# Cross-covariance attention and channel mix: all engines in a hand-written, step-by-step woven order

## The chip, the cores and the metric

One core of one Trainium2 chip. The metric is the device time of one execution in microseconds (us). All runs that are quoted were fast (none was over 1.5% above the fastest of its kernel). The granted clock is the share of its full clock that PE was given, as the profile records it. PE is the matrix engine (TensorE), PEld its weight loads, ACT ScalarE, DVE VectorE, POOL GpSimd.

## The reference, cut to what matters

Four batches of 6208 tokens with 256 channels; the hidden width of the channel mix is 1024.

```python
# attention over channels: q, k, v are [4, 6208, 256]
qn = q / (norm(q, axis=1, keepdims=True) + 1e-6)      # norm over tokens
kn = k / (norm(k, axis=1, keepdims=True) + 1e-6)
a  = softmax(kn.transpose(0, 2, 1) @ qn / tau)        # [4, 256, 256]
x  = v @ a
# channel mix with a token shift
x_prev = x shifted by one token, 0 in front
xk = mu_k * x + (1 - mu_k) * x_prev;  xr = mu_r * x + (1 - mu_r) * x_prev
k  = maximum(xk @ w_k, 0)                             # "up", 256 -> 1024
v  = (k * k) @ w_v                                    # "down", 1024 -> 256
out = sigmoid(xr @ w_r) * v
```

A batch must have its whole covariance (q, k) and its softmax before its first x. So a batch's covariance is made while the blocks of the batch before it run through the channel mix.

## The kernel before

Each batch has 12 blocks of 512 tokens; the 64 tokens left over in each batch are treated together, once. The order below is what is *written*. The framework's scheduler then decides in which order each engine runs it, within the dependencies.

```python
def cov_group(b, g):                       # 512 tokens of q and k: one "group of rows"
    ...
    if b == 0:                             # first batch: f32 loads, cast on DVE
        qk_f = pq.tile([P, S, 2, C], F32, name="qk_f", tag="qk_f")      # 4 buffers
        for i in range(2):
            nc.sync.dma_start(qk_f[:rows, :n, i, :], src[i])            # 1 KB pieces
        nc.vector.tensor_copy(qk[:rows, :n], qk_f[:rows, :n])
        nc.scalar.activation(qk2[:rows, :n], qk_f[:rows, :n], AF.Square)
    else:                                  # later batches: casting software loads (POOL)
        for i in range(2):
            nc.gpsimd.dma_start(qk[:rows, :n, i, :], src[i])
        nc.scalar.activation(qk2[:rows, :n], qk[:rows, :n], AF.Square)  # 2048 columns
    for s in range(n):                     # one "row": 1024 matmul columns
        nc.tensor.matmul(ssq_ps, ones[:rows], qk2[:rows, s]..., ...)
        for ih in range(2):
            nc.tensor.matmul(s_ps[:, ih, :], qk[:rows, s, 1, ...], qk[:rows, s, 0, :], ...)

def channel_mix(xk, xr, m, store):
    for fh in range(8):                    # up
        kT_ps = ps.tile([P, M], F32, name="kT_ps", tag="kT_ps", bufs=2)
        for dh in range(2):
            nc.tensor.matmul(kT_ps[:, :m], w_k_sb[...], xk[:, dh, :m], ...)
        if fh == 7:
            nc.vector.tensor_relu(kr[:, :m], kT_ps[:, :m])
        else:
            nc.scalar.activation(kr[:, :m], kT_ps[:, :m], AF.Relu)
        nc.vector.tensor_tensor(kk[:, fh, :m], kr[:, :m], kr[:, :m], op=OP.mult)
    for s in range((m + P - 1) // P):      # down and gate
        vr_ps = ps.tile([P, 2 * D], F32, name="vr_ps", tag="vr_ps", bufs=2)
        # 2 matmuls with w_r_sb, 8 with w_v_sb
        nc.scalar.activation(res[:ms, s], vr_ps[:ms, D:], AF.Sigmoid)
        nc.vector.tensor_tensor(res[:ms, s], res[:ms, s], vr_ps[:ms, :D], op=OP.mult)
    store(res)

for g in range(NB + 1):
    cov_group(0, g)
load_weights()
...
cov_softmax(0)
for i, (b, t) in enumerate(blocks):
    ...
    project(b, vs.pop(i), xT, carry)       # transposes of v, x = v @ a
    xk, xr = mix(xT, M)
    if b + 1 < B and t < NB - 1:
        cov_group(b + 1, t)                # next batch's rows
        ...
    channel_mix(xk, xr, M, store_block(b, t))
    if b + 1 < B and t == NB - 2:
        cov_softmax(b + 1)
```

Of the kernel before, what the change touches and what calls it, by code (L numbers as in the profile page):

```python
# [10 lines left out]
F32 = mybir.dt.float32  # L11
# [7 lines left out]
def kernel(  # L19
# [31 lines left out]
    ps = ctx.enter_context(tc.tile_pool(name="ps", bufs=1, space=bass.MemoryType.PSUM))  # L51

# [12 lines left out]
    a_sb = const.tile([P, B, 2, C], BF16, name="a_sb")  # L65

    def load_weights():
        nc.sync.dma_start(mu_k_t, moe_mu_k.rearrange("(h p) -> p h", p=P))
        nc.sync.dma_start(mu_r_t, moe_mu_r.rearrange("(h p) -> p h", p=P))
        nc.gpsimd.dma_start(w_k_sb, moe_w_k.rearrange("(ko ki) f -> ki ko f", ki=P))  # L70
        nc.gpsimd.dma_start(w_r_sb, moe_w_r.rearrange("(ko ki) d -> ki ko d", ki=P))
        nc.gpsimd.dma_start(w_v_sb, moe_w_v.rearrange("(fo fi) d -> fi fo d", fi=P))


    cov = {}

    def cov_group(b, g):

        if g == 0:
            cov[b] = (ps.tile([P, 2, C], F32, name="s_ps", tag="s_ps"),  # L80
                      ps.tile([P, 2 * C], F32, name="ssq_ps", tag="ssq_ps"))
        s_ps, ssq_ps = cov[b]
        full = g < NB
        n = S if full else 1
        rows = P if full else L
        src = []
        for t in (q, k):
            if full:
                src.append(t[b, :NB * M, :].rearrange("(p j) c -> p j c", p=P)[:, g * S:(g + 1) * S, :])
            else:  # L90
                src.append(t[b, NB * M:, :].rearrange("(p j) c -> p j c", j=1))
        qk = pq.tile([P, S, 2, C], BF16, name="qk", tag="qk")
        qk2 = pq.tile([P, S, 2, C], BF16, name="qk2", tag="qk2", bufs=3)
        if b == 0:
            qk_f = pq.tile([P, S, 2, C], F32, name="qk_f", tag="qk_f")
            for i in range(2):
                nc.sync.dma_start(qk_f[:rows, :n, i, :], src[i])  # L97
            nc.vector.tensor_copy(qk[:rows, :n], qk_f[:rows, :n])  # L98
            nc.scalar.activation(qk2[:rows, :n], qk_f[:rows, :n], AF.Square)
        else:  # L100
            for i in range(2):
                nc.gpsimd.dma_start(qk[:rows, :n, i, :], src[i])  # L102
            nc.scalar.activation(qk2[:rows, :n], qk[:rows, :n], AF.Square)
        for s in range(n):
            t0 = g == 0 and s == 0
            te = g == NB
            nc.tensor.matmul(ssq_ps, ones[:rows], qk2[:rows, s].rearrange("p i c -> p (i c)"),  # L107
                             start=t0, stop=te)
            for ih in range(2):
                nc.tensor.matmul(s_ps[:, ih, :], qk[:rows, s, 1, ih * P:(ih + 1) * P],  # L110
                                 qk[:rows, s, 0, :], start=t0 and ih == 0, stop=te,
                                 skip_group_check=True)

    def cov_softmax(b):
        s_ps, ssq_ps = cov.pop(b)
        nrm = pn.tile([P, 2 * C], F32, name="nrm")
        nc.scalar.activation(nrm, ssq_ps, AF.Sqrt)
        junk = pn.tile([P, P], F32, name="junk")
        rk = pn.tile([P, 2], F32, name="rk")
        for ih in range(2):  # L120
            nc.vector.scalar_tensor_tensor(junk, nrm[:, C + ih * P:C + (ih + 1) * P], 1.0, ident_f,
                                           op0=OP.mult, op1=OP.mult, accum_out=rk[:, ih:ih + 1])
        nc.vector.tensor_scalar_add(nrm[:, :C], nrm[:, :C], 1e-6)
        rq = pn.tile([P, C], F32, name="rq")
        nc.vector.reciprocal(rq, nrm[:, :C])
        nc.vector.tensor_scalar_add(rk, rk, 1e-6)
        nc.vector.reciprocal(rk, rk)
        if inv_tau != 1.0:
            nc.vector.tensor_scalar_mul(rk, rk, inv_tau)
        s_sb = pn.tile([P, 2, C], F32, name="s_sb")  # L130
        nc.vector.tensor_tensor(s_sb, s_ps, rq.unsqueeze(1).to_broadcast([P, 2, C]), op=OP.mult)
        for ih in range(2):
            nc.vector.tensor_scalar_mul(s_sb[:, ih], s_sb[:, ih], rk[:, ih:ih + 1])
        mx = pn.tile([P, 2], F32, name="mx")
        nc.vector.tensor_reduce(mx, s_sb, axis=AX, op=OP.max, negate=True)
        sm = pn.tile([P, 2], F32, name="sm")
        for ih in range(2):
            nc.scalar.activation(s_sb[:, ih], s_sb[:, ih], AF.Exp, bias=mx[:, ih:ih + 1],
                                 accum_out=sm[:, ih:ih + 1])
        nc.vector.reciprocal(sm, sm)  # L140
        for ih in range(2):
            nc.vector.tensor_scalar_mul(a_sb[:, b, ih, :], s_sb[:, ih], sm[:, ih:ih + 1])


    def load_v(b, t):
        v_bf = p2.tile([P, S, C], BF16, name="v_bf", tag="v_bf", bufs=4)
        nc.gpsimd.dma_start(v_bf, v[b, t * M:(t + 1) * M, :].rearrange("(s p) c -> p s c", p=P))  # L147
        return v_bf

    def mix(xT, m):  # L150

        delta = p2.tile([P, 2, M], BF16, name="delta", tag="delta")
        xk = p2.tile([P, 2, M], BF16, name="xk", tag="xk")
        xr = p2.tile([P, 2, M], BF16, name="xr", tag="xr")
        nc.vector.tensor_tensor(delta[:, :, :m], xT[:, :, 1:m + 1], xT[:, :, :m], op=OP.subtract)  # L155
        for mu, o in ((mu_k_t, xk), (mu_r_t, xr)):
            for dh in range(2):
                nc.vector.scalar_tensor_tensor(o[:, dh, :m], delta[:, dh, :m], mu[:, dh:dh + 1],  # L158
                                               xT[:, dh, :m], op0=OP.mult, op1=OP.add)
        return xk, xr  # L160

    def project(b, v_bf, xT, carry):

        vT_ps = ps.tile([P, 2, M], BF16, name="vT_ps", tag="vT_ps")
        for ch in range(2):
            for s in range(S):
                nc.tensor.transpose(vT_ps[:, ch, s * P:(s + 1) * P], v_bf[:, s, ch * P:(ch + 1) * P], ident)  # L167
        vT = p2.tile([P, 2, M], BF16, name="vT", tag="vT", bufs=2)
        nc.vector.tensor_copy(vT, vT_ps)  # L169
        for dh in range(2):  # L170
            xT_ps = ps.tile([P, M], F32, name="xT_ps", tag="xT_ps")
            for ih in range(2):
                nc.tensor.matmul(xT_ps, a_sb[:, b, ih, dh * P:(dh + 1) * P], vT[:, ih, :],  # L173
                                 start=ih == 0, stop=ih == 1)
            nc.scalar.copy(xT[:, dh, 1:], xT_ps)  # L175
        if carry is None:
            nc.gpsimd.memset(xT[:, :, 0:1], 0.0)
        else:
            nc.gpsimd.tensor_copy(xT[:, :, 0:1], carry)  # L179

    def channel_mix(xk, xr, m, store):
        kk = p2.tile([P, 8, M], BF16, name="kk", tag="kk", bufs=2)
        for fh in range(8):
            kT_ps = ps.tile([P, M], F32, name="kT_ps", tag="kT_ps", bufs=2)
            for dh in range(2):
                nc.tensor.matmul(kT_ps[:, :m], w_k_sb[:, dh, fh * P:(fh + 1) * P], xk[:, dh, :m],  # L186
                                 start=dh == 0, stop=dh == 1)
            kr = p2.tile([P, M], BF16, name="kr", tag="kr", bufs=4)
            if fh == 7:
                nc.vector.tensor_relu(kr[:, :m], kT_ps[:, :m])  # L190
            else:
                nc.scalar.activation(kr[:, :m], kT_ps[:, :m], AF.Relu)  # L192
            nc.vector.tensor_tensor(kk[:, fh, :m], kr[:, :m], kr[:, :m], op=OP.mult)  # L193
        res = p2.tile([P, S, D], F32, name="res", tag="res")
        for s in range((m + P - 1) // P):
            ms = min(P, m - s * P)
            vr_ps = ps.tile([P, 2 * D], F32, name="vr_ps", tag="vr_ps", bufs=2)
            for dh in range(2):
                nc.tensor.matmul(vr_ps[:ms, D:], xr[:, dh, s * P:s * P + ms], w_r_sb[:, dh, :],  # L199
                                 start=dh == 0, stop=dh == 1)  # L200
            for fh in range(8):
                nc.tensor.matmul(vr_ps[:ms, :D], kk[:, fh, s * P:s * P + ms], w_v_sb[:, fh, :],  # L202
                                 start=fh == 0, stop=fh == 7)
            nc.scalar.activation(res[:ms, s], vr_ps[:ms, D:], AF.Sigmoid)  # L204
            nc.vector.tensor_tensor(res[:ms, s], res[:ms, s], vr_ps[:ms, :D], op=OP.mult)  # L205
        store(res)


    L1 = L + 1
    xl = const.tile([P, 2, B, L1], BF16, name="xl")  # L210

    def project_left(b):
# [105 lines left out]
```

## Time and profile before

| | before |
|---|---|
| device time, median of 3 (range) | 675.58 us (672.81 to 677.64) |
| span of the profile, mean granted clock | 673.3 us, 0.974 |
| estimate of the pure matmul stream | 528 us |
| last cast of the first batch's rows, a_sb of batch 0 | 59.9, 74.0 us |
| first up-projection matmul | 88.75 us |
| first Sigmoid to first Sigmoid, 12 blocks from block 12 on | 144.9 us |

The matmul stream is an estimate from the trace: 3912 matmuls stream about 1.243 million columns, and where nothing waits they start 109 ns apart with 256 columns and 216 ns apart with 512. So 673.3 - 528 = 145 us of the span are not streaming. Until its first up matmul PE had about 37.5 us of work (estimate from the same spacings over the 282 matmuls recorded before it), so 51 of the 145 us are lost at the start and 94 us after it.

The head of the page of the kernel before: busy time, then 40 equal slices of the span in tenths.

```profile
span 673.3 us, 10691 instructions
...
PE 594.1 (88%) x3912; PEld 362.1 (54%) x3912; DVE 476.3 (71%) x1008; ACT 423.4 (63%) x730; POOL 121.4 (18%) x187
...
PE   2676798999998789999998699999998899989886
...
PEclk9997899999999789999998899999998999999999
...
GB/s 225 286 304 210 176 139 82 45 121 66 74 115 160 107 141 32 91 133 35 125 81 133 152 67 117 71 88 89 120 79 16 79 79 79 63 86 40 33 63 62
```

PE looks 88% busy, but a 512-column matmul is recorded as some 380 ns where one can start every 216 ns, so a gap of one matmul does not show as idle. The Trainium skill says so too ("Perfetto Trace Analysis", Identifying the Most-Contended Engine): matmul busy time is a poor measure; the busy share of the weight loads, beside the share of peak FLOPs, is a better one. Here the weight loads are busy 54% of the span.

The start, as DVE sees it (timeline of DVE before: start, duration, line and operation, and in brackets how long the engine had been idle and what released it):

```profile
45.38 1.23 DVE L98 CAST qk<-qk_f 128x2048 bf16<-128x2048 f32 x1 [3.17 <-DMA qk_f<-in_k_dram]
51.46 1.23 DVE L98 CAST qk<-qk_f 128x2048 bf16<-128x2048 f32 x1 [4.86 <-DMA qk_f<-in_k_dram]
55.43 1.23 DVE L98 CAST qk<-qk_f 128x2048 bf16<-128x2048 f32 x1 [2.73 <-DMA qk_f<-in_k_dram]
58.72 1.56 DVE L98 CAST qk<-qk_f 128x2048 bf16<-128x2048 f32 x2 [2.07 <-DMA qk_f<-in_k_dram]
```

The casts wait for the loads of the rows. The last row is two casts: the last full group at 58.72 and the last 64 rows at 59.9. Weights, v and the next batch's rows load at the same time. Then ACT (timeline of ACT before) puts Squares of the *next* batch's rows between the Sqrt and the Exp of the first softmax:

```profile
62.45 0.60 ACT L117 ACTIVATE nrm<-ssq_ps 128x512 f32<-128x512 f32 x1
62.95 1.90 ACT L103 ACTIVATE qk_407<-qk 128x2048 bf16<-128x2048 bf16 x1
65.92 1.91 ACT L103 ACTIVATE qk_558<-qk 128x2048 bf16<-128x2048 bf16 x1 [1.07 <-DMA qk<-in_k_dram]
69.49 1.91 ACT L103 ACTIVATE qk_709<-qk 128x2048 bf16<-128x2048 bf16 x1 [1.65 <-DMA qk<-in_k_dram]
71.42 1.28 ACT L138 ACT_TABLE_LOAD   x1
```

In the later part the costliest groups of the page (busy, mean ns of one, idle time just before them and what ended most of it) show PE waiting for what ACT and DVE make of its results:

```profile
L186 PE MATMUL kT_ps<-xk,w_k_sb 128*128 128x512 bf16 (+1 forms) x784 | 219.6, 379 | 11.9 <-ACT kr L192 9.6
...
L202 PEld LDWEIGHTS <-kk 128*128 128x128 bf16 x1552 | 144.6, 98 | 70.7 <-DVE kk L193 28.4
...
L199 PE MATMUL vr_ps<-w_r_sb,xr 128*128 128x256 bf16 x388 | 80.0, 276 | 11.3 <-DVE res L205 10.1
```

### The profile page before, as it was taken

Reading aid. Unit: us, or ns where it says so; the run is one execution under the profiler, and the core shown is the slowest. Engines: PE = TensorE matmul, PEld = TensorE weight load, DVE = VectorE, ACT = ScalarE, POOL = GpSimd, SP = SyncE. Lnnn points to the kernel's source line nnn. Section 1 sums busy time; section 2 is a strip of 40 time slices with the busy share of each in tenths; the row PEclk is TensorE's granted clock in tenths of the full one; section 3 lists DMA queues with packets and bytes.
Section 4 is the critical chain, followed back from the end, with each engine's and each line's share of the span. In section 5 each row is a group of like instructions: output and inputs, shape, how many; then the busy total and the mean of one; then the engine's idle time right before and its main releaser. Section 6 shows DMA issues by size and latency. Waiting matters only on the chain.

```text
span 673.3 us, 10691 instructions
## 1 busy us (share of the span) xinstructions
PE 594.1 (88%) x3912; PEld 362.1 (54%) x3912; DVE 476.3 (71%) x1008; ACT 423.4 (63%) x730; POOL 121.4 (18%) x187
## 2 busy tenths in 40 slices
PE   2676798999998789999998699999998899989886
PEld 1343465656655346666665365665564465655554
DVE  1234077898786358979776489877767888887874
ACT  2346696566587656666668666657656756556553
POOL 3013431100134120220214210023110101010000
PEclk9997899999999789999998899999998999999999
DMA  9999993162379690371739936255631424141011
GB/s 225 286 304 210 176 139 82 45 121 66 74 115 160 107 141 32 91 133 35 125 81 133 152 67 117 71 88 89 120 79 16 79 79 79 63 86 40 33 63 62
DMA packets 104900, 71.80 MB, mean 107 GB/s; under 512 B 3980, under 2 KB 104592, under 8 KB 104848
## 3 DMA queue, kind: packets, MB, share of 16 engines
q0 software_dynamic: 65808, 32.98, 39.1%
q1 hardware_dynamic: 39040, 38.15, 17.3%
q8 instruction: 30, 0.49, 0.3%
q14 instruction: 22, 0.18, 0.1%
HBM read 78.65 MB, written 25.43 MB: 155 GB/s over the span
## 4 chain that ended last, share of the span: by engine, by line
PE 58%; DMA 13%; DVE 10%; issue 8%; ACT 6%; SPq 2%; POOL 1%; ACTq 0%; DVEq 0%; POOLq 0%
PE kT_ps L186 20%; PE vr_ps L202 20%; DMA qk<-in_k_dram 8%; DMA qk_f<-in_k_dram 6%; PE xT_ps L173 5%; PE vr_ps L199 5%; PE ssq_ps L107 3%; PE s_ps L110 3%; DVE xk L158 2%; DVE kk L193 2%; ACT kr L192 2%; DVE xr L158 2%; SPq L97 2%; PE vT_ps L167 2%; ACT xT L175 2%
## 5 line engine op out<-in xcount | busy, mean ns | idle before, releaser
L202 PE MATMUL vr_ps<-w_v_sb,kk 128*128 128x256 bf16 x1552 | 232.6, 274 | 1.6 <-DVE kk L193 1.0
L186 PE MATMUL kT_ps<-xk,w_k_sb 128*128 128x512 bf16 (+1 forms) x784 | 219.6, 379 | 11.9 <-ACT kr L192 9.6
L192 ACT ACTIVATE kr<-kT_ps 128x512 bf16<-128x512 f32 (+1 forms) x343 | 190.5, 597 | 54.1 <-PE kT_ps L186 48.7
L202 PEld LDWEIGHTS <-kk 128*128 128x128 bf16 x1552 | 144.6, 98 | 70.7 <-DVE kk L193 28.4
L193 DVE TENSOR_TENSOR kk<-kr 128x512 bf16<-128x512 bf16 (+1 forms) x392 | 155.1, 417 | 27.9 <-ACT kr L192 21.3
L204 ACT ACTIVATE res<-vr_ps 128x256 f32<-128x256 f32 x194 | 69.2, 384 | 94.7 <-PE vr_ps L202 93.3
L205 DVE TENSOR_TENSOR res<-res,vr_ps 128x256 f32<-128x256 f32 x194 | 76.2, 415 | 73.4 <-ACT res L204 73.3
L186 PEld LDWEIGHTS <-w_k_sb 128*128 128x128 bf16 x784 | 76.3, 98 | 78.5 <-issue 37.8
L110 PE MATMUL s_ps<-qk 128*128 128x256 bf16 x392 | 79.2, 302 | 30.7 <-DVE qk L98 26.2
L199 PE MATMUL vr_ps<-w_r_sb,xr 128*128 128x256 bf16 x388 | 80.0, 276 | 11.3 <-DVE res L205 10.1
L175 ACT CAST xT<-xT_ps 128x512 bf16<-128x512 f32 x96 | 57.2, 596 | 28.7 <-PE xT_ps L173 27.0
L110 PEld LDWEIGHTS <-qk 128*128 128x128 bf16 x392 | 40.2, 107 | 63.4 <-DVE qk L98 29.8
L173 PE MATMUL xT_ps<-vT,a_sb 128*128 128x512 bf16 x192 | 63.0, 382 | 9.8 <-ACT xT L175 6.1
L158 DVE SCALAR_TENSOR_TENSOR xk<-delta,mu_k_t,xT 128x512 bf16<-128x512 bf16 x96 | 69.6, 746 | 0.8
L158 DVE SCALAR_TENSOR_TENSOR xr<-delta,mu_r_t,xT 128x512 bf16<-128x512 bf16 x96 | 69.7, 743 | 0.0
L147 POOL DMA_DIRECT2D v_bf<-in_v_dram x48 | 35.9, 751 | 176.7 <-PE vT_ps L167 60.8
L179 POOL COPY xT<-xT 128x2 bf16<-128x2 bf16 x44 | 23.6, 537 | 217.3 <-issue 106.9
L199 PEld LDWEIGHTS <-xr 128*128 128x128 bf16 x388 | 36.6, 98 | 33.6 <-issue 9.5
L169 DVE COPY vT<-vT_ps 128x1024 bf16<-128x1024 bf16 x48 | 32.9, 685 | 25.4 <-PE xT_ps L173 14.0
L102 POOL DMA_DIRECT2D qk<-in_q_dram x39 | 29.6, 758 | 92.3 <-issue 39.5
L98 DVE CAST qk<-qk_f 128x2048 bf16<-128x2048 f32 (+1 forms) x13 | 15.6, 1208 | 40.2 <-DMA qk_f<-in_k_dram 36.9
L155 DVE TENSOR_TENSOR delta<-xT 128x1024 bf16<-128x1024 bf16 x48 | 33.1, 689 | 7.6 <-ACT xT L175 6.5
(150 smaller groups left out, 406.3 us busy)
## 6 DMA issues: line engine op xcount, KB each, us to landing
out_dram<-res SPq DMA_DIRECT2D x48, 512.0 KB, 3.0
v_bf<-in_v_dram POOLq DMA_DIRECT2D x48, 256.0 KB, 5.3
qk<-in_q_dram POOLq DMA_DIRECT2D x36, 256.0 KB, 5.2
qk<-in_k_dram POOLq DMA_DIRECT2D x36, 256.0 KB, 6.6
qk_f<-in_q_dram SPq DMA_DIRECT2D x12, 512.0 KB, 12.0
qk_f<-in_k_dram SPq DMA_DIRECT2D x12, 512.0 KB, 12.0
w_k_sb<-in_moe_w_k_dram POOLq DMA_DIRECT2D x1, 512.0 KB, 9.0
w_v_sb<-in_moe_w_v_dram POOLq DMA_DIRECT2D x1, 512.0 KB, 14.8
```

The costliest lines, as they stand in the source:

```text
L110: nc.tensor.matmul(s_ps[:, ih, :], qk[:rows, s, 1, ih * P:(ih + 1) * P], qk[:rows, s, 0, :], start=t0 and ih == 0, stop=te, skip_group_che ...
L147: nc.gpsimd.dma_start(v_bf, v[b, t * M:(t + 1) * M, :].rearrange("(s p) c -> p s c", p=P))
L158: nc.vector.scalar_tensor_tensor(o[:, dh, :m], delta[:, dh, :m], mu[:, dh:dh + 1], xT[:, dh, :m], op0=OP.mult, op1=OP.add)
L173: nc.tensor.matmul(xT_ps, a_sb[:, b, ih, dh * P:(dh + 1) * P], vT[:, ih, :], start=ih == 0, stop=ih == 1)
L175: nc.scalar.copy(xT[:, dh, 1:], xT_ps)
L186: nc.tensor.matmul(kT_ps[:, :m], w_k_sb[:, dh, fh * P:(fh + 1) * P], xk[:, dh, :m], start=dh == 0, stop=dh == 1)
L192: nc.scalar.activation(kr[:, :m], kT_ps[:, :m], AF.Relu)
L193: nc.vector.tensor_tensor(kk[:, fh, :m], kr[:, :m], kr[:, :m], op=OP.mult)
L199: nc.tensor.matmul(vr_ps[:ms, D:], xr[:, dh, s * P:s * P + ms], w_r_sb[:, dh, :], start=dh == 0, stop=dh == 1)
L202: nc.tensor.matmul(vr_ps[:ms, :D], kk[:, fh, s * P:s * P + ms], w_v_sb[:, fh, :], start=fh == 0, stop=fh == 7)
L204: nc.scalar.activation(res[:ms, s], vr_ps[:ms, D:], AF.Sigmoid)
L205: nc.vector.tensor_tensor(res[:ms, s], res[:ms, s], vr_ps[:ms, :D], op=OP.mult)
```

## The change

The intent: the scheduler is switched off, and the order of every engine is written by hand, so that PE always has a matmul whose operands were made at least a step ago. An iteration has eight steps. A step has one up pair of block i+1, five down matmuls of block i, and in some steps x of block i+2, transposes of v for block i+3, or one covariance row of the next batch. The softmax of a new batch is cut in seven pieces, one per step.

At the start, q and k go to separate f32 tiles, so that a partition's piece of a load is 4 KB and not 1 KB, with six buffers each; and a tiny copy on POOL (`gate`) holds back all software loads until the tenth group is cast. Squares of later batches are cut in four, and the eighth Relu moves from DVE to ACT. Matmuls and bytes stay the same.

```diff
+    ctx.enter_context(tc.manual_schedule())
     ...
+                f = pq.tile([P, S, C], F32, name=f"f{i}", tag=f"f{i}", bufs=6)
+                nc.sync.dma_start(f[:rows, :n], qk_src(t, b, g))
     ...
+    def unit_square(b, g, s):
+        nc.scalar.activation(qk2[:rows, s], qk[:rows, s], AF.Square)      # 512 columns
     ...                                       (softmax_pieces: a, b1, b2, c, d, e, f)
+    for g in range(NB + 1):
+        group_load(0, g)
+        group_cast(0, g)
+        for s in range(rows_of(g)[1]):
+            unit_matmul(0, g, s)
+        if g == NB - 3:
+            nc.gpsimd.tensor_copy(gate, groups[0, g][0][:, 0, 0, 0:1])
+            ...                               (loads of mu, v and w_k)
     ...                                       (more loads, v_transpose 0 and 1, softmax of batch 0)
+    for i in range(-2, NBLK):
+        for j in range(8):
+            if j % 2 == 0:
+                ...                           finish(i, j // 2 - 1): Sigmoid, product, store
+            if chain:
+                chain.pop(0)()                # one softmax piece
+            if 0 <= i + 1 < NBLK:
+                up(i + 1, j)                  # 2 matmuls, Relu
+            ...                               square(i + 1, j - 1): kk on DVE
+            if i >= 0:
+                down(i, j)                    # 5 matmuls
+            if i + 2 < NBLK:
+                ...                           j 0, 2: x_half; j 3: mix_delta; j 4, 5, 7: mix
+            ...                               j 1: mix xr of i+1; j 6: v_transpose(i + 3); j 7: v_evac
+            if j in (1, 3, 4, 5, 7) and ...:
+                unit()                        # one covariance row of the next batch
+            ...                               left rows: left_x
```

## The prediction

> **What bounds it now.** The page gives a span of 673.3 us, PE busy 88%, DVE 71%, ACT 63%. The PE figure hides gaps, because a 512-column matmul is recorded as 381 ns. In the timeline, dense matmuls start every 109 ns (256 columns) and 216 ns (512); this agrees with the gap N/2.4 + 2.5 ns of the Trainium skill, "TensorE: Matmul & The Clock Gate", Back-to-back issue gap. The program streams about 1.243 million columns in 3912 matmuls, so 518 + 10 = 528 us at full clock (estimate from that spacing). 145 us are lost, in three places:
> - Start: the first up-projection matmul starts at 88.7 us. Until then PE had about 33 us of work (13 groups of 1.75 us, 6 of the next batch). The casts of the first batch's rows come 3.06 us apart when their loads run alone and 6.1 us apart while weights, v or the next rows load too (DVE timeline); the last comes at 58.7 us. Exp then waits behind three 1.9 us Squares, a_sb is ready only at 74.8, x only at 83.8.
> - Batch changes: 208-256 and 352-384 us have PE gaps, granted clock 0.84-0.94, and waits on q/k loads.
> - Elsewhere about 7%: 16 us windows hold 110 matmuls, about 14.9 us of streaming. Waits: PE for kk, for kT_ps (two banks), for vr_ps.
>
> **What the change does.** Same matmuls and bytes. The order is fixed: each of 8 steps per block has one up pair of block i+1, five down matmuls of block i, and in some steps x, transposes or one covariance row of 1024 columns. Operands are made about one step (1.0-1.4 us) or more ahead. A step with a covariance row streams 3328 columns, 1.41 us; a block with five rows takes 11.3 us of PE, one without 9.1 us (estimates).
> Other engines, with the slots seen when they run back to back (Relu or copy 0.5 us, Sigmoid 0.3, kk 0.34, xk/xr 0.67, delta and vT 0.61, res 0.33): ACT about 6.2 us per block, plus 2.6 for five Squares (cut in four, and Relu 7 moved from DVE: both cost ACT time); DVE about 7.9 us. Both fit under PE; DVE is tight (87%) in blocks without rows, and there I expect small PE waits for vT.
> The start: software loads are held back until the tenth group is cast, rows come in contiguous 4 KB pieces. Last cast near 47 us; softmax without Squares in front, a_sb near 57; first up near 62, first down near 71. Its new risk is that w_k, v and four row groups then queue together.
>
> **Sum.** First down 71; 28 blocks of 11.3 and 20 of 9.1 give 499; stalls of 3.5% 17; softmax boundaries 3 x 2 us (table loads of 1.28 us on ACT); leftovers and tail about 4. About **597 us**, 12% less. Range 8 in 10: 580 to 622. Faster by over 2%: 0.94; within 2%: 0.04; slower: 0.02. Nearly all of it is on the critical path, because PE is the chain in the steady part.
>
> **What would show it.** First kT_ps matmul at 58-66 us instead of 88.7; blocks of 11.3-11.7 us with rows and 9.3-9.7 without (from output stores); granted clock 1.0 across batch changes; PE waits on kk, kT_ps and vr_ps nearly gone; the tally of PE work unchanged; ACT busy up, DVE down slightly.
>
> **What would make it wrong.** A strict order has no slack for a late operand: if ACT runs over 1.4 us per step, or DVE falls behind in blocks without rows, every step stretches (10 us a block is +17 us). If carry copies on POOL wait behind loads, x is late at the start. If the held-back loads end late, the start saves only 10 us.

## The result, and the profile after

| | before | after |
|---|---|---|
| device time, median (range) | 674.42 us (4 runs of the same rounds) | 593.83 us (593.47 to 593.95, 4 runs) |
| ratio, 95% interval | | 0.8799 (0.8763 to 0.8835) |
| span, mean granted clock | 673.3, 0.974 | 592.1, 0.982 |
| last cast, a_sb of batch 0 | 59.9, 74.0 | 37.0, 47.2 |
| first up matmul, first down matmul | 88.75, 90.04 | 54.50, 62.61 |
| span minus the stream of 528 us | 145 | 64 |
| of these before the first up matmul | 51 | 29 |
| 12 blocks from block 12 on | 144.9 | 139.8 |

Every ratio here is the mean time of one kernel's fast runs over that of the other's fast runs of the same rounds, so not quite the ratio of the medians. The 29 us are 54.5 us minus the 25 us of work that PE has before that point after the change (estimate from the spacings, counted by weight loads because some matmul records are missing).

The same lines of the page, after:

```profile
span 592.1 us, 10699 instructions
...
PE 541.9 (92%) x3842; PEld 367.3 (62%) x3912; DVE 440.0 (74%) x972; ACT 457.1 (77%) x895; POOL 126.5 (21%) x188
...
PE   5857999999889999999969999999977999999996
...
PEclk9996999999889999999999999999999999999999
...
GB/s 331 413 257 197 144 105 174 95 90 149 83 37 142 156 112 127 141 97 116 98 54 175 95 124 100 171 94 62 100 55 54 100 63 109 70 93 72 37 73 89
```

The work of PE is unchanged (3912 weight loads; 70 matmul records are missing from this trace). Its weight loads are busy 62% of the span instead of 54%. The PE row has four dips: the start, and the three batch changes in slices 11 and 12, 21, and 30 and 31.

The start after (three lines of DVE's timeline, then one of PE's):

```profile
35.92 0.97 DVE L103 CAST qk<-f_345 128x1024 bf16<-128x1024 f32 x1 [0.87 <-DMA f_345<-in_k_dram]
...
40.98 1.75 DVE L144 RECIPROCAL rq<-nrm 128x256 f32<-128x256 f32 x1
...
47.19 0.63 DVE L171 TENSOR_SCALAR a_sb<-s_sb,sm 128x256 bf16<-128x256 f32 x2
```

```profile
54.50 1.02 PE L273 MATMUL kT_ps<-xk,w_k_sb 128*128 128x512 bf16 x2
```

The first up matmul is 34.2 us earlier. The last cast gives 22.9 of them (59.9 to 37.0), the softmax, from that cast to a_sb, 4.0 (14.2 to 10.2), and the way from a_sb to the up matmul 7.4 (14.7 to 7.3).

The groups of the page after that answer to those shown of before:

```profile
L273 PE MATMUL kT_ps<-xk,w_k_sb 128*128 128x512 bf16 (+1 forms) x750 | 226.4, 380 | 10.2 <-ACT kr L276 8.6
...
L301 PEld LDWEIGHTS <-kk 128*128 128x128 bf16 x1552 | 152.5, 98 | 60.3 <-issue 1.4
...
L297 PE MATMUL vr_ps<-w_r_sb,xr 128*128 128x256 bf16 x388 | 74.6, 274 | 0.9 <-issue 0.2
```

The waits for kk and for res are gone. The wait of the up matmuls for a Relu is nearly as long as before, 8.6 us, but it now comes in 8 places instead of 18, all of them at the batch changes. The three at the first change are shown below, and the same 1.60 and 1.05 us come again at the second (at 305.66 and 307.84) and at the third.

One step of the steady part and the start of the next (timeline of PE after):

```profile
201.06 0.59 PE L273 MATMUL kT_ps<-xk,w_k_sb 128*128 128x512 bf16 x2
201.49 0.38 PE L297 MATMUL vr_ps<-w_r_sb,xr 128*128 128x256 bf16 x2
201.71 0.49 PE L301 MATMUL vr_ps<-w_v_sb,kk 128*128 128x256 bf16 x3
202.04 0.61 PE L197 MATMUL vT_ps<-ident,v_bf 128*128 128x128 bf16 x8
202.48 0.59 PE L273 MATMUL kT_ps<-xk,w_k_sb 128*128 128x512 bf16 x2
```

No bracket: PE waits for nothing, and each group starts when the one before has streamed (3 down matmuls from 201.71 to 202.04, 110 ns each). From first Sigmoid to first Sigmoid such a block takes 11.30 us with five covariance rows and 9.14 us without. These are the two figures that the estimate of the pure stream gives. The blocks of before are uneven: in the last batch they alternate 14.89 and 7.57, 22.46 us for two, against 18.28 now.

The first Sigmoid comes 33 us earlier (100.3, now 67.4). From it on, the three batches that have a next one took 155.0, 144.9 and 144.6 us per 12 blocks and now take 139.6, 139.8 and 134.3; the rest took 128.5 and now takes 111.0. So the loop gains 48 us, and the batch in the table is the one that gains least.

What is still lost sits at the batch changes. The first one, three timelines after (PE, ACT, DVE):

```profile
154.63 0.59 PE L273 MATMUL kT_ps<-xk,w_k_sb 128*128 128x512 bf16 x2 [0.33 <-ACT kr L276]
...
157.83 1.01 PE L218 MATMUL xT_ps<-vT,a_sb 128*128 128x512 bf16 x2 [2.06 <-DVE vT L202]
...
165.99 0.59 PE L273 MATMUL kT_ps<-xk,w_k_sb 128*128 128x512 bf16 x2 [1.60 <-ACT kr L276]
...
168.18 0.58 PE L273 MATMUL kT_ps<-xk,w_k_sb 128*128 128x512 bf16 x1 [1.05 <-ACT kr L276]
```

```profile
152.20 1.28 ACT L140 ACT_TABLE_LOAD   x1
153.49 0.60 ACT L140 ACTIVATE nrm<-ssq_ps 128x512 f32<-128x512 f32 x1
...
163.08 1.28 ACT L165 ACT_TABLE_LOAD   x1
...
165.96 1.28 ACT L309 ACT_TABLE_LOAD   x1
```

```profile
154.49 1.75 DVE L144 RECIPROCAL rq<-nrm 128x256 f32<-128x256 f32 x1
156.16 0.36 DVE L282 TENSOR_TENSOR kk<-kr 128x512 bf16<-128x512 bf16 x1
156.44 0.74 DVE L258 SCALAR_TENSOR_TENSOR xr<-delta,mu_r_t,xT 128x512 bf16<-128x512 bf16 x1
157.09 0.68 DVE L202 COPY vT<-vT_ps 128x1024 bf16<-128x1024 bf16 x1
```

In the fixed order the copy of vT stands behind the reciprocal of 1.75 us, and x waits 2.06 us for it. Between 163.08 and 167.25 ACT has two table loads and two Exps around a single Relu, and the up matmuls wait for their Relus. After the longest wait here PE also runs at half clock (busy time by stretch of the span; the two last figures before DMA and GB/s are POOL's busy time and the granted clock):

```profile
155.00:158.00 3.00, 0.94 (x8) 0.59 (x6) 3.00 (x5) 2.22 (x4) 0.00 (x0) 0.96 0.75 87
158.00:161.00 3.00, 3.00 (x11) 1.34 (x10) 2.86 (x11) 1.39 (x3) 0.00 (x0) 0.50 0.50 178
```

The clock stays at 0.50 from 157.8 to 161.2 us and again from 168.0 to 171.4. The same waits do not always bring this: at the second change PE also waits 2.06 us for vT and the clock stays at 1.00 (it falls only after the later waits, from 307.9 to 311.4), and at the third, with a wait of 2.01 us, it does not fall at all.

The two blocks of the three batch changes take 14.59 + 13.98, 13.53 + 13.81 and 13.00 + 13.72 us. With three covariance rows in the first of them and none in the second, streaming would take 9.14 + 3 x 0.43 + 9.14 = 19.6 us. So the changes lose 9.0, 7.8 and 7.2 us, 24 us in all.

### The profile page after: what moved, and what is told of

The parts are those of the page before. It is cut to its first block, busy times and chain, and to the rows that moved or that the text cites. A ratio compares the mean times of both kernels' runs of the same rounds, so it can differ in the third digit from the quotient of the medians.

```text
span 592.1 us, 10699 instructions
## 1 busy us (share of the span) xinstructions
PE 541.9 (92%) x3842; PEld 367.3 (62%) x3912; DVE 440.0 (74%) x972; ACT 457.1 (77%) x895; POOL 126.5 (21%) x188
## 5 line engine op out<-in xcount | busy, mean ns | idle before, releaser
L276 ACT ACTIVATE kr<-kT_ps 128x512 bf16<-128x512 f32 (+1 forms) x392 | 232.4, 595 | 64.1 <-PE kT_ps L273 24.3
L273 PE MATMUL kT_ps<-xk,w_k_sb 128*128 128x512 bf16 (+1 forms) x750 | 226.4, 380 | 10.2 <-ACT kr L276 8.6
L301 PEld LDWEIGHTS <-kk 128*128 128x128 bf16 x1552 | 152.5, 98 | 60.3 <-issue 1.4
L282 DVE TENSOR_TENSOR kk<-kr 128x512 bf16<-128x512 bf16 (+1 forms) x392 | 151.0, 414 | 2.3 <-ACT kr L276 2.3
L310 DVE TENSOR_TENSOR res<-res,vr_ps 128x256 f32<-128x256 f32 x194 | 81.3, 419 | 94.5 <-ACT res L309 94.0
L309 ACT ACTIVATE res<-vr_ps 128x256 f32<-128x256 f32 x194 | 74.1, 382 | 3.0 <-PE vr_ps L301 2.3
L297 PE MATMUL vr_ps<-w_r_sb,xr 128*128 128x256 bf16 x388 | 74.6, 274 | 0.9 <-issue 0.2
L213 POOL COPY xT<-xT 128x2 bf16<-128x2 bf16 x44 | 27.9, 635 | 221.2 <-issue 177.5
L218 PE MATMUL xT_ps<-vT,a_sb 128*128 128x512 bf16 x181 | 55.8, 385 | 14.4 <-DVE vT L202 8.0
L189 POOL DMA_DIRECT2D v_bf<-in_v_dram x48 | 36.2, 755 | 118.8 <-DVE kk L282 79.8
L97 POOL DMA_DIRECT2D qk<-in_q_dram x39 | 28.9, 741 | 60.8 <-PE s_ps L122 10.1
L197 PE MATMUL vT_ps<-ident,v_bf 128*128 128x128 bf16 x384 | 30.2, 223 | 1.0 <-DVE nrm L143 1.0
```

The source lines that it names most:

```text
L189: nc.gpsimd.dma_start(v_bf, v[b, t * M:(t + 1) * M, :].rearrange("(s p) c -> p s c", p=P))
L218: nc.tensor.matmul(xT_ps, a_sb[:, b, ih, dh * P:(dh + 1) * P], vT[:, ih, :], start=ih == 0, stop=ih == 1)
L273: nc.tensor.matmul(kT_ps[:, :m], w_k_sb[:, dh, fh * P:(fh + 1) * P], xk[:, dh, :m], start=dh == 0, stop=dh == 1)
L282: nc.vector.tensor_tensor(st[i, "kk"][:, fh, :m], kr[:, :m], kr[:, :m], op=OP.mult)
L297: nc.tensor.matmul(vr_ps[:, D:], xr[:, dh, s * P:(s + 1) * P], w_r_sb[:, dh, :], start=dh == 0, stop=dh == 1)
L301: nc.tensor.matmul(vr_ps[:, :D], kk[:, fh, s * P:(s + 1) * P], w_v_sb[:, fh, :], start=fh == 0, stop=fh == 7)
```

## The experiments

Twelve kernels ran in three jobs, each kernel in three rounds beside the kernel before (medians of before: 674.65, 675.22 and 675.29 us). All results were correct. The theory was: PE streams everything that it is given, and the fixed order is what lets it; the start gains by the held loads and the bigger pieces. The rivals: the woven *written* order is what matters, and a scheduler does as well with it; or the gain is nearly all in the start.

| kernel | median us | ratio to before (95%) |
|---|---|---|
| after (its own rounds) | 593.83 | 0.8799 (0.8763 to 0.8835) |
| nogate | 599.24 | 0.8883 (0.8824 to 0.8941) |
| kb1 | 599.97 | 0.8895 (0.8842 to 0.8949) |
| auto | 587.55 | 0.8707 (0.8660 to 0.8754) |
| before_manual | 1036.01 | 1.5343 (1.5261 to 1.5424) |
| space | 590.88 | 0.8751 (0.8703 to 0.8798) |
| coarse | 669.38 | 0.9908 (0.9855 to 0.9962) |
| coarse_auto | 611.72 | 0.9057 (0.9008 to 0.9107) |
| mix | 576.23 | 0.8528 (0.8472 to 0.8583) |
| tanh | 727.90 | 1.0765 (1.0708 to 1.0821) |
| tanh_mix | 733.81 | 1.0846 (1.0798 to 1.0895) |
| start_only | 666.70 | 0.9860 (0.9811 to 0.9909) |
| sq1 | 605.38 | 0.8948 (0.8907 to 0.8989) |

### nogate: the software loads are not held back

```diff
-            nc.gpsimd.tensor_copy(gate, groups[0, g][0][:, 0, 0, 0:1])
```

> The changed kernel without the small copy that holds the software loads back; all else the same. Theory (holding back lets the first batch's rows have the DMA engines alone): v of blocks 0 and 1 and w_k, 1 MB as bf16, share the engines with the first rows, the last cast moves from 37 us to 41-44, the first up-projection matmul from 54.5 to 58-61, and the time rises by 3 to 6 us. Rival (the bytes before the first block are the same, so their order does not matter): within 1.5 us.

Measured: 599.24 us, 5.4 us more than after. The last full group is cast at 41.6 us instead of 35.9, and the first up matmul comes at 59.5 instead of 54.5. The shift of the start is the shift of the whole time. Holding the loads back is worth about 5 us.

### kb1: 1 KB pieces again, six buffers kept

```diff
-                f = pq.tile([P, S, C], F32, name=f"f{i}", tag=f"f{i}", bufs=6)
+                if i == 0:
+                    f2 = pq.tile([P, S, 2, C], F32, name="f", tag="f", bufs=6)
+                f = f2[:, :, i, :]
```

> The changed kernel with q and k of a first-batch group put side by side in one tile again, so that each row piece in SBUF is 1 KB, not 4 KB, as in the kernel before; loads still held back. Theory (piece size sets the rate at which the first rows land: 3.06 us a group in the kernel before with nothing else loading, 2.5 us in the changed one): groups come about 3.06 us apart, the last cast moves by 5 to 7 us, the time by +5 to +7 us. Rival (2.5 us comes from more buffers and no contention, not from piece size): within 1.5 us.

Measured: 599.97 us, 6.1 us more. Undisturbed groups of rows are cast 2.74 us apart (13.96 to 30.40 us for six) instead of 2.52, the last full one at 42.0 us instead of 35.9, and the first up matmul comes at 61.2. The rate alone makes 12 x 0.22 = 2.6 us; the rest comes at the end, where the last full cast waits 3.77 us for its load. The edit also puts q and k in one tile, so that their buffer comes free only when both are used. Pieces and separate tiles together are worth about 6 us; this run does not part them.

### auto: the woven order as written, left to the scheduler

```diff
-    ctx.enter_context(tc.manual_schedule())
```

> The changed kernel without the manual schedule: the same instructions, tiles and buffers, emitted in the same order, but the scheduler may place them. Theory (the order itself gives the steady gain of about 50 us): blocks lose their even 11.3 and 9.1 us, PE waits on kk, kT_ps and vr_ps come back, 615 to 655 us. Rival (the rewriting of buffers, loads and emission order is enough, and the scheduler would find as good an order): below 603 us.

Measured: 587.55 us, 6 us *less* than after. The theory, that the fixed order is what brings the gain, fell with this run. The start is much worse: the first Sigmoid comes at 84.7 us instead of 67.4. The scheduler put transposes of v into PE's queue before rows of the first batch, and PE, which took them in that order, waited there for the loads of v (one line of the waits of auto: total, times, longest):

```profile
PE vT_ps L196 <- DMA v_bf<-in_v_dram: 21.9, 3, 13.0
```

The loop, though, gives it all back: the 12 blocks from block 12 on take 133.4 us against 139.8 in after. Steady blocks are as fast in both (11.30 and 9.13); the batch changes are shorter.

### before_manual: the order written before, fixed

```diff
+    ctx.enter_context(tc.manual_schedule())       # the only line added to the kernel before
```

> The kernel before with the manual schedule switched on and nothing else changed: every engine follows its program order, block after block. Theory (what helps is the weave, not that order is fixed): PE waits in each block for x and its mixes, about 5 us a block, 760 to 860 us. Rival (the scheduler's choices are the harm, and any fixed order is better): below 670 us.

Measured: 1036.01 us at a mean clock of 0.847. The direction was expected, the size was not. In this order ACT waits 218 us for kT_ps, and the expectation had not counted the lower clock. The comparison of the four kernels so far says that what is *written* decides, and not who has the last word: with the order of before, fixing it costs 361 us; with the woven order, fixing it costs 6. But the two programs differ in more than their order (loads, buffers, cut Squares, the eighth Relu), and this comparison does not part these.

### space: the softmax pieces further apart

```diff
+    SLOTS = {(7, 6), (8, 0), (8, 1), (8, 3), (8, 6), (9, 0), (9, 2)}
-            if chain:
+            if chain and (i % NB, j) in SLOTS:
```

> The changed kernel with the seven softmax pieces of a batch change spread over 12 steps instead of 7 (the 1.75 us reciprocal after, not just before, the copy of vT that x needs); same instructions. Theory (the 9 us that each of the three batch changes loses come from long softmax pieces put too densely into an order that can't move around them): PE's 2.1 us wait for vT goes, the two slowest blocks of a change sum to 24-26 us instead of 28.6, the time falls by 8 to 14 us. Rival (the four table loads of a change are the cost, wherever they stand): within 4 us of the changed kernel.

Measured: 590.88 us, 3 us less than after. The first change takes 13.65 + 12.90 us instead of 14.59 + 13.98. The waits moved rather than went: PE now waits 1.73 us for kk at 158.91 and 2.14 us for vT at 169.06. The expected 8 to 14 us did not come. The time is in the rival's range, within 4 us, but this does not show the rival's cause, the table loads: both waits named here end with DVE work. That each piece is longer than a step's slack wherever it stands is a reading of these waits, not a test.

### coarse and coarse_auto: the eight up pairs of an iteration together

```diff
-            if 0 <= i + 1 < NBLK:
-                up(i + 1, j)
-            ...
+            if j == 0:
+                ...
+                for jj in range(8):
+                    if 0 <= i + 1 < NBLK:
+                        up(i + 1, jj)
+                        if jj > 0:
+                            square(i + 1, jj - 1)
```

coarse_auto has the same edit and no `manual_schedule`.

> The changed kernel with the eight up steps of block i+1 put in front of the rest of the iteration, all still in fixed order. Theory (the step-by-step weave is needed, because ACT takes about 0.5 us per up pair and PE 0.43, with two banks, while ACT has little to do during the down matmuls): PE waits for kT_ps in each up stretch, blocks of 12.3-13 and 10.2-11 us, 635 to 680 us. Rival (only the distance of one block between up and down matters): within 10 us of the changed kernel.

> The same with the scheduler free to place instructions. Theory (the emission order is the scheduler's priority, so it cannot recover the weave): over 610 us. Rival (the scheduler finds the weave whatever the order of emission inside an iteration, once up runs a block ahead of down): below 600 us, near the 587.6 us of the woven order with the scheduler.

Measured: coarse 669.38 us, the same as before within 2%, with the whole new start still in it. Blocks take 12.65 us with rows and 10.80 without, 1.35 and 1.66 more than woven. One iteration's up pairs in coarse (timeline of PE):

```profile
210.99 1.03 PE L273 MATMUL kT_ps<-xk,w_k_sb 128*128 128x512 bf16 x4
212.27 1.08 PE L273 MATMUL kT_ps<-xk,w_k_sb 128*128 128x512 bf16 x4 [0.25 <-ACT kr L276]
213.54 2.40 PE L273 MATMUL kT_ps<-xk,w_k_sb 128*128 128x512 bf16 x8 [0.20 <-ACT kr L276]
215.79 0.38 PE L297 MATMUL vr_ps<-w_r_sb,xr 128*128 128x256 bf16 x2
```

The 16 matmuls take 215.79 - 210.99 = 4.80 us where streaming takes 16 x 0.216 = 3.46: PE streams a pair in 0.43 us, but with two buffers of kT_ps the next pair can come only when a Relu of some 0.6 us has cleared one, and pairs come 0.60 us apart. The difference, 1.34 us, is the whole loss of a block with rows. So the weave works by putting 0.55 us of down matmuls (and at times a row) between two pairs.

coarse_auto: 611.72 us, blocks of 11.78 and 9.93 us. Given the coarse order, the scheduler gets back 0.87 of the 1.35 us in each block, but not all. It too depends on the order in which the work is written.

The run also limits what the step-by-step weave explains. From its first Sigmoid (87.5 us) on, coarse_auto takes 522 us, where before takes 573 and after 525 (12 blocks from block 12 on: 138.5, 144.9 and 139.8). So with the scheduler a loop as fast as that of after comes without this weave. What after and coarse_auto have in common against before (up a block ahead of down, rows spread over the blocks, the softmax in pieces, cut Squares, buffers, the eighth Relu) brings that together; no run here parts it.

### mix: fixed start, loop left to the scheduler

```diff
-    ctx.enter_context(tc.manual_schedule())
+    start = _ES()
+    start.enter_context(tc.manual_schedule())
     ...
     left_go = {}
+    start.close()
     for i in range(-2, NBLK):
```

> The changed kernel with the fixed order ended after the start (first batch's covariance, held loads, first softmax), and the loop left to the scheduler. Theory (the fixed order helps only in the start, where the scheduler put transposes that wait 13 us for v into the PE queue, and harms at the batch changes): first Sigmoid near 67-69 us as in the changed kernel, batch changes as in the scheduler's run, 567 to 575 us. Rival (the scheduler's loop needs its own start, or its gain at the batch changes came from the later start): 583 us or more.

Measured: 576.23 us (574.68 to 576.47), ratio 0.8528. That is just above the expected range, and 17.6 us faster than after: a version that beats both kernels. But the start did not stay as expected: a_sb comes at 52.9 us (47.2 in after) and the first Sigmoid at 73.3, not at 67 to 69. The scheduler put ten Squares of the next batch's rows between the first Sqrt and the first Exp, and DVE waited 7.0 us for that Exp. The 12 blocks from block 12 on take 133.4 us, as in auto; streaming alone would take 12 x 9.14 + 49 x 0.43 = 130.8. The DVE timeline of mix at the first batch change shows what the scheduler does there:

```profile
155.04 0.69 DVE L204 COPY vT<-vT_ps 128x1024 bf16<-128x1024 bf16 x1 [0.17 <-PE vT_ps L199]
...
156.26 1.75 DVE L146 RECIPROCAL rq<-nrm 128x256 f32<-128x256 f32 x1
157.93 0.36 DVE L284 TENSOR_TENSOR kk<-kr 128x512 bf16<-128x512 bf16 x1
```

The copy of vT goes ahead of the reciprocal, and covariance rows of the next batch are pulled forward as filling for PE. All four table loads are still there; PE's waits in this stretch are 0.15 to 0.33 us, and its clock is 1.00.

### tanh and tanh_mix: no change of tables, and why this settled nothing

The norms by a power of -0.5 on POOL, and the Sigmoid as 0.5 (1 + tanh), so that one table serves the whole program (tanh in the order of space, tanh_mix in that of mix).

```diff
-            nc.scalar.activation(nrm, ssq_ps, AF.Sqrt)
+            nc.vector.tensor_copy(nrm, ssq_ps)
     ...
-            nc.vector.reciprocal(rq, nrm[:, :C])
+            nc.gpsimd.tensor_tensor(rq, nrm[:, :C], half, op=OP.pow)      # half is -0.5
     ...
-        nc.scalar.activation(kr[:, :m], kT_ps[:, :m], AF.Relu)
+        nc.scalar.activation(kr[:, :m], kT_ps[:, :m], AF.Relu, scale=0.5 ** 0.5)
     ...
-        nc.scalar.activation(res[:, s], vr_ps[:, D:], AF.Sigmoid)
-        nc.vector.tensor_tensor(res[:, s], res[:, s], vr_ps[:, :D], op=OP.mult)
+        nc.scalar.activation(res[:, s], vr_ps[:, D:], AF.Tanh, scale=0.5)
+        nc.vector.scalar_tensor_tensor(res[:, s], res[:, s], 1.0, vr_ps[:, :D], op0=OP.add, op1=OP.mult)
```

> The changed kernel, fixed order, with the softmax pieces spread as in the run before last and all ACT functions from one table: the norms' root and reciprocal by a power of -0.5 on POOL, Sigmoid as Tanh of half the argument (its factor 0.5 put into the Relu's scale). Theory (after the spacing run: table loads, 4 x 1.28 us per batch change, block ACT for longer than the one step of slack): the two slowest blocks of a change go from 28.6 (26.6 when spread) to 20-22 us, waits of PE for kT_ps go, 565 to 574 us. Rival (softmax work on DVE, on top of a block that is 87% full, holds PE): 582 us or more.

> The same without table loads, with the fixed order for the start only and the scheduler's in the loop. Theory (the scheduler already hides most of the loads by moving work around them; what is left is the start and about 2 us a batch): 2 to 6 us under the 576.2 us of the fixed-start run, 568 to 574 us. Rival (the loads cost the scheduler's loop as much as the fixed one): 556 us or less.

Measured: 727.90 and 733.81 us, slower than before. Both theories failed, since the substitute costs far more than what it replaced (groups of tanh: line, busy, mean ns of one):

```profile
L145 POOL TENSOR_TENSOR rq<-nrm,half 128x256 f32<-128x256 f32 x4 | 165.4, 41358 | 30.8 <-DVE nrm L142 30.7
```

One power of 128x256 values took 41.4 us on POOL, and DVE waited 153.8 us for the four. What a batch change would cost without table loads stays open.

### start_only: the kernel before with the new loads of the start

```diff
-            qk_f = pq.tile([P, S, 2, C], F32, name="qk_f", tag="qk_f")
+                f = pq.tile([P, S, C], F32, name=f"f{i}", tag=f"f{i}", bufs=5)
     ...
+        held(w_k_sb[:, 0, 0:1])          # the same for w_r, w_v and the first four v_bf
     ...
+    def held(t):                          # hold[0] is the qk of the tenth group
+        nc.gpsimd.tensor_copy(t, hold[0][:, 0, 0, 0:1])
```

> The kernel before with the start of the changed one alone: 4 KB row pieces, five buffers each, weights and the first v held back until the tenth group is cast; the loop untouched. Theory (the start is worth about 28 us by itself, and the loop the other 53): last cast from 58.7 to 38-43 us, first up-projection matmul from 88.7 to 60-72 us, 643 to 660 us. Rival (the loop was late for other reasons, so an earlier start is given back): over 668 us.

Measured: 666.70 us, 8.6 us less than before and within 2% of it. The last full group was cast at 37.7 us, 21 us earlier than before, so the loads do what they do in after. But the last 64 rows were cast only at 45.6: transposes of v stood in PE's queue and waited 7.65 us for their held load, and the copy of their result stood on DVE in front of that cast. a_sb came at 63.5 and the first up matmul only at 79.8, against an expected 60 to 72. From the last cast to the up matmul nothing was gained either (34.2 us, before 28.9): DVE waited 8.9 us for the Exp, which stood behind other work of ACT, and rows of the next batch, one of them a wait of 4.12 us for its load, stood in PE's queue ahead of x. So the start's gain is the loads *and* an order in which softmax, x and up come first.

### sq1: one Square of 1.9 us per group, fixed order

```diff
-        nc.scalar.activation(qk2[:rows, s], qk[:rows, s], AF.Square)
+        if s == 0:
+            nc.scalar.activation(qk2[:rows, :n], qk[:rows, :n], AF.Square)
```

> The changed kernel with one Square of 1.9 us for each group of four covariance rows, as in the kernel before, in place of four of 0.6 us; the rest, with the fixed order, the same. Theory (an ACT operation longer than a step breaks a fixed order): PE waits for kT_ps or for the squares at each of 36 groups, 0.5 to 1 us each, 610 to 632 us. Rival (two banks and four kr buffers absorb it): within 3 us of the changed kernel.

Measured: 605.38 us, 11.5 us more than after; on average 0.3 us for each of 36 groups of rows. But 3.4 us of it come before the first Sigmoid and 4.7 at the batch changes, and only the rest in the steady blocks. The direction was the theory's, the size under its range. Blocks with rows are 11.30 us where the long Square falls well and up to 13.17 where it does not. An ACT instruction longer than a step of 1.41 us shows up on PE here, but in the steady blocks by little; that the two and four buffers absorb the rest is argued, not tested.

## Why the prediction was right or wrong, point by point

The total was right: 593.83 us measured, 597 predicted, range 580 to 622. The sum behind it was right in its largest terms and wrong in three smaller ones that cancel; that the total came within 1% is luck.

- **Right: the bound.** PE's stream bounds the steady part. The predicted 11.3 and 9.1 us for a block were measured as 11.30 and 9.14, with clock 1.00. Blocks without rows did not even show the 9.3 to 9.7 that it allowed for output stores. In the fixed order the weave is what lets PE do this: coarse, the same work with the up pairs together, loses 1.35 us a block to the pace of the Relus.
- **Mis-sized: "stalls of 3.5% 17".** There are none in the steady blocks. The fear of a tight DVE in blocks without rows ("there I expect small PE waits for vT") did not come true; the waits for vT in the list are 8.0 us in 5 places in the whole program, the longest the 2.06 us of the batch change.
- **Mis-sized: "softmax boundaries 3 x 2 us".** They cost 9.0, 7.8 and 7.2 us, 24 instead of 6. The prediction counted the time of the table loads. It did not ask what the fixed order puts *behind* each piece: at the first change the waits shown add up to 0.33 + 2.06 + 1.60 + 1.05 = 5.0 us, and two stretches of 3.4 us at clock 0.50 lose up to another 3.4. It had also said that the clock would be 1.0 across batch changes, and that the waits for kT_ps would nearly go. At the three changes PE waits 8.6 us for Relus of ACT and 7.4 us for vT of DVE.
- **Mis-sized: the start.** First up "near 62" came at 54.5, first down "71" at 62.6, because the last cast came at 37.0 and not near 47: the loads ran at 2.52 us per group. nogate and kb1 moved the last full cast by 5.7 and 6.1 us.
- **The sum.** Start 8.4 us earlier, 17 us of stalls absent, 18 us more at the batch changes, and 2.5 us more elsewhere: 597 - 8.4 - 17 + 18 + 2.5 = 592, the span. Left rows are in the last term; a block that has them takes 12.33 us instead of 11.30.
- **Wrong as a belief, though not in the sum: that the fixed order is the gain.** auto and mix show that the scheduler, given the woven order, makes the same steady blocks and better batch changes. What the fixed order is good for is the start, where it keeps transposes that wait for late loads out of PE's queue: mix against auto, 11 us.
- **Not settled:** which part of the rewriting brings the loop's 48 us when a scheduler has the last word (coarse_auto has about as fast a loop without the step-by-step weave; buffers and the eighth Relu were never changed alone). And how the 24 us of the batch changes divide between table loads on ACT and the long pieces on DVE: the waits above end with both engines. space moved 3 us; the run without table loads failed for another reason. mix, with all its table loads, shows only that most of the 24 us can be avoided by order alone: a batch of 12 blocks costs 6.4 us less than in after.

## What to carry to other kernels

In a fixed order, interleave at the grain at which the slowest helper keeps up: one pair of matmuls whose result costs another engine 0.6 us needs matmuls of other work between it and the next pair, and here the program written in that order also ran 24 us faster than the coarse one when the scheduler had the last word. Fix the order by hand only where an in-order queue would otherwise get a wait for late data in front of ready work, as at the start here; elsewhere compare the fixed order with the scheduler on the same written order before keeping it. Before fixing an order, list every instruction about as long as a step or longer (here, with steps of 1.0 to 1.4 us, the 1.75 us reciprocal, the 1.28 us table loads, the 1.9 us Square) and see what stands right behind each.

## What the Trainium skill lacked or had wrong

- "TensorE: Matmul & The Clock Gate", Back-to-back issue gap: the page's formula, N/2.4 + 2.5 ns, fits (109 and 216 ns measured for 256 and 512 columns). It presents this as the isolated gap, and gives 131 ns at 512 columns and 81 ns at 128 as the sustained spacing with weight loads. Here sustained streams with a weight load for every matmul ran at 216 ns, and eight transposes of 128 columns at 55 ns each (202.04 to 202.48 us).
- The same page, Why this matters for your kernels, asks for no PE-idle gaps over about 3 us to keep the clock up. Here one idle stretch of 2.06 us was followed by a granted clock of 0.50 for the next 3 us, and 1.60 + 1.05 us close together by 0.50 as well. At the third batch change waits of 2.01, 1.60 and 1.05 us were not (clock 1.00 from 436 to 452 us). The page's remark that the observation window runs freely would allow such scatter; no run here tests it.
- "ScalarE: Activation LUTs", What ACT_TABLE_LOAD costs: 1283 ns for the load agrees (1.28 us). The drain of about 1380 ns that the page adds, for 2.66 us in all, does not show: the load starts at 152.20 us, 0.01 us after the activation before it has ended, and the next one starts at 153.49, so a switch cost 1.29 us.
- "DMA: Bandwidth & Descriptors", Where 436 GB/s comes from: about 358 GB/s per core is said to bind loads from HBM, though the page's own table has 425 GB/s for one core alone. Here, with one core, the second slice of the span after moved 413 GB/s, and two loads of 512 KB came every 2.52 us (estimate: 416 GB/s). The page's minimum for line rate is 512 B; pieces of 1 KB per partition, into a joined tile, were slower than pieces of 4 KB, 2.74 against 2.52 us per pair of loads.
- "GPSIMD Engine Reference" has no figure for a power. A tensor_tensor power of 128x256 f32 values took 41.4 us there.
